# First group of attention without whole query products: the first queries' heads on both row halves, half steps from score 8

## The chip, the cores and the metric

One core of one Trainium2 chip runs the whole program. The metric is device time in microseconds, the median of timed runs. The engines are PE (TensorE: matrix products, with weight loads listed as PEld), ACT (ScalarE), DVE (VectorE), POOL (GpSimd) and SP (SyncE, which here only issues transfers). Each works through its own instructions in order, and they wait for each other by semaphores.

## The reference

A pre-LayerNorm block with multi-query attention (32 heads of 16, one shared key and value head) and a gated feed-forward part:

```python
def _A_ref(x, wq, wk, wv, wo):
    q = (x @ wq).reshape(B, S, H, Dh).transpose(0, 2, 1, 3)
    k = x @ wk
    v = x @ wv
    scores = jnp.einsum("bhqd,bkd->bhqk", q, k) * (Dh ** -0.5)
    p = _softmax(scores, axis=-1)
    o = jnp.einsum("bhqk,bkd->bhqd", p, v)
    return o.transpose(0, 2, 1, 3).reshape(B, S, H * Dh) @ wo

def _B_ref(x, w_gate, w_up, w_down):
    return (_gelu(x @ w_gate) * (x @ w_up)) @ w_down

h = x + _A_ref(_layernorm(x), A_wq, A_wk, A_wv, A_wo)
h2 = h + _B_ref(_layernorm(h), B_w_gate, B_w_up, B_w_down)
```

S is 2048 tokens, D 512, F 1792, everything in float32.

## The kernel before

**Tiling.** The 2048 queries are four blocks of 512 (`b`), the 32 heads are eight groups of four (`g`), the keys sixteen chunks of 128 (`kc`). A *score* is the work of one call of `score(n)`: for two heads, keys of one chunk against 512 queries, two products on PE (L411) into one PSUM tile `s`, followed by one exponential of 128x1024 on ACT (L415) that writes half of a tile `p`. So a group has 32 scores, a block 256; `n` counts them through the program. Two scores (four heads) make one *weighing*: four products with the values into the accumulator `acc` (L419). After a group's last weighing DVE copies `acc` to `oT` (L432), SP stores it to `acc_d` and loads it back in another layout as `oc` (L445), and DVE divides and splits it into `o_hi` and `o_lo`. There is one `acc` bank, and there are three banks for `s`: two with tag `s`, and one, `s3`, for every third score. A score therefore waits for the exponential of three scores earlier.

**Rows.** A product here has only 50 rows of depth: each head's queries are split into a high and a low float32r part, three times 16 rows, plus a row with a bound on the exponent and a row of zeros. `kaug` holds the keys' counterpart twice, in rows 0 to 49 and 64 to 113, so two heads go through the two halves of PE's rows at the same time. Queries take the way through DRAM: `project_q(b, cs, ...)` computes `x @ wq` for 128 columns (eight heads) in PSUM (`pq`), DVE or ACT split it into `qh` and `ql`, SP writes these to `q_d` (L253), and `load_q` reads four heads' 50 rows into `qg` (L391). For block 0 `load_q` puts all four heads into both halves of the rows. The very first group has its own tile `qg_first` (`first_q`, L350, and `first_bound`, L361): heads 0 and 2 in rows 0 to 49, heads 1 and 3 in rows 64 to 113, and nothing in the other halves.

**Projections beside scores.** A projection of 128 columns is 12 *whole products* (four chunks of depth, three terms), or 24 *half steps*, each on 64 of the 128 rows. `scores(..., beside)` (L399) takes two half steps: each goes to one half of the rows, while one head's score product goes through the other half. `project_q` yields `(lane, left, step)` for half steps: first the twelve of lane 0 (rows 0 to 63), then, after DVE has read a mark from the bank, the twelve of lane 1. All products of one projection share one bank `pq` (`psum1`, one buffer in this stage), which DVE copies to `pq_raw` at the end.

**Order.** PE, POOL, ACT, DVE and SP follow the order in which the code is written in this stage. `run` begins group 0 in a loop of its own (from L1064): before certain scores, listed in `RAMP` and then before every fourth, it takes whole products from `later_q`, whose first part is `project_q(1, range(DC), nc.vector, 1, (0, 1))`: columns 0 and 1 of block 1 as whole products, the rest as half steps. In between `q_rest` finishes block 0's own projections (columns 1 to 3: split, store, sums of squares `pqn`, bound `m`). When both are done, a second loop (from L1076) runs plain scores up to score 31 and follows the table `MIXED` from score 32 on: in a period of ten scores, `m` marks one with half steps beside it and `s` a plain one, in runs `mms`, `smm`, `mm`, `ss`, with one or two weighings after each run. `left` counts the half steps still to come and `LAST_Q` (240) the score by which they shall be done.

**Weights.** Beside this `part_weights` goes through 46 pieces of `wo`, `w_gate`, `w_up` and `w_down`: SP loads one (L519), POOL splits it into a high and a low part (L121, L122) and stores both to DRAM (L528, L534). There are four buffers for what is loaded and two for what is stored. At score 256 the early buffers are given up, and SP loads `wo` for the dense part (`load_wo`, L584); this waits for all that still uses those buffers, POOL's stores included. From score 272 on the dense part (projection `pp`, gate, up, down) is woven into the scores of the next block.

Of the kernel before, what the change touches and what calls it, by code (L numbers as in the profile page):

```python
# [9 lines left out]
F32 = mybir.dt.float32  # L10
# [24 lines left out]
LAST_Q = 240  # L35
# [4 lines left out]

HURRY = ((0, 3), (1, 0), (1, 1))

RAMP = {3: 2, 5: 2, 7: 2}

MIXED = {0: ("mms", 2), 3: ("smm", 1), 6: ("mm", 1), 8: ("ss", 1)}

# [4 lines left out]
CUT, EDGE, GAP, HOLD, REST = -1, -2, -3, -4, -5  # L51
# [3 lines left out]
def kernel(  # L55
# [12 lines left out]
    nc = tc.nc  # L68
# [6 lines left out]
    T = 512  # L75
    NT = S // P
    NB = S // T
    TB = T // P
    DC = D // P
    FC = F // P  # L80
    NG = H // 4
    KC = S // P
    HC = P // DH
    KR = 3 * DH + 2
# [25 lines left out]
    q_d = dram.tile([H, KR, S], F32R, name="q_d")  # L110
# [49 lines left out]
    def run(outer, first):  # L160
# [157 lines left out]
        q_rest = project_q(0, range(FIRST_Q, DC), nc.scalar, NB)  # L318

        def later_q():  # L320

            second = project_q(1, range(DC), nc.vector, 1, (0, 1))
            for _ in range(sum(RAMP.values())):
                yield next(second)

            next(q_rest)
            for _ in range(2 * DC - sum(RAMP.values())):
                yield next(second)
            yield from q_rest
            yield 0  # L330
            yield from second
            for b in range(2, NB):
                yield from project_q(b, range(DC), nc.vector, b, ())
            yield REST
            yield REST
            norms.pop()()

        def age():
            for entry in after:
                entry[0] -= 1  # L340
            while after and after[0][0] <= 0:
                after.pop(0)[1]()

        def first_q():

            qg = eb.tile([P, 4, T], F32R, name="qg_first")
            view = q_d.rearrange("h r s -> r h s")
            for a in range(2):
                for r0, r1 in ((3 * DH + 1, KR), (0, 3 * DH)):
                    nc.sync.dma_start(  # L350
                        qg[64 * a + r0 : 64 * a + r1, a::2, :].bitcast(F32),
                        view[r0:r1, a:4:2, :T].bitcast(F32),
                    )
            return qg

        def first_bound(qg):

# [642 lines left out]
        work = None  # L1000
        qgs = {(0, 0): qg_first if first else load_q(0, 0)}
        acc = None
        pend = []

        def finish(n):
            for _ in range(min(n, len(pend))):
                pb, pg, pkc, pp, pacc, _ = pend.pop(0)
                weigh(pacc, pp, pkc)
                if pkc == KC - 1:
                    evacuate(pb, pg, pacc)  # L1010
# [17 lines left out]
        def score(n, beside=()):  # L1028

            nonlocal acc  # L1030
            i, u = divmod(n, 2)
            b, r = divmod(i, PER)
            g, kc = divmod(r, KC)
            if u == 0:
                if kc == 0:
                    cur["qg"] = qgs.pop((b, g))
                    acc = pss.tile([P, T], F32, tag="acc", bufs=1, name=f"acc_{b}_{g}")
                if kc == 2 and b * NG + g + 1 < NB * NG:
                    key = divmod(b * NG + g + 1, NG)
                    qgs[key] = load_q(*key)  # L1040
                cur["p"] = sb.tile([P, 4, T], F32, tag="p", bufs=PB, name=f"p_{i}")
            scores(i, cur["p"], cur["qg"], kc, u, beside)
            if u == 1:
                pend.append((b, g, kc, cur["p"], acc, n))
# [11 lines left out]
        LEAD = (3, 2, 2)  # L1056
        n, lead = 0, 2 * PER + sum(SIZES[: LEAD[0]])
        with tc.manual_schedule(engines={mybir.EngineType.SP, mybir.EngineType.DVE}):
            parts, said = None, 3 if first else 0
            if first:  # L1060
                work = later_q()
                parts = part_weights(early.enter_context(tc.tile_pool(name="parts", bufs=1)))

            while n < 2 * KC and said:  # L1064
                for _ in range(RAMP.get(n, n > 7 and n % 4 == 3) if said else 0):
                    said = next(work)
                    age()
                score(n)
                n += 1
                if n % 4 == 0:  # L1070
                    finish(len(pend) - 2)
                    if parts is not None and n > 12 and n % 24:
                        next(parts)

            token, left = next(work) if first else None, 6 * (NB * DC - 2 - DC) * DC
            while n < lead:  # L1076
                age()
                r = n % (2 * KC)
                if n < 2 * KC or token is None and n % 2 == 0:
                    kinds, runs = "ss", 1  # L1080
                elif r < 30:
                    kinds, runs = MIXED[r % 10]
                else:
                    kinds, runs = ("mm" if left > LAST_Q - n else "ss"), 1
                rest, held = token == REST, False
                if n == 2 * PER:
                    assert token is None
                    while after:
                        age()
                    for _ in parts or ():  # L1090
                        pass
                    if first:
                        check_bound(eb, k2m)
                    parts = work = None
                    early.close()
                    db = late.enter_context(tc.tile_pool(name="dense", bufs=1))
                    load_wo(0)
                for kind in kinds:
                    if kind == "m" and not rest and not held and token not in (None, REST):
                        held = token[1] == 1  # L1100
                        tokens = token, next(work)
                        score(n, [(lane, step) for lane, _, step in tokens])
                        token = next(work, None)
                        left -= 2
                    else:
                        score(n)
                    n += 1
                if n == 2 * PER + 8:
                    primed = dense(0)
                    next(primed)  # L1110
                if rest:
                    token = next(work, None)
                if len(pend) > 2:
                    finish(runs)
                while squares:
                    squares.pop(0)()
                for _ in range(runs):
                    if outs and not pause[0] and n % (2 * KC) not in (2, 3, 4):
                        take_out()
                    pause[0] = max(pause[0] - 1, 0)  # L1120
                if parts is not None and (
                    n % (2 * KC) % 10 in (0, 6) if n > 2 * KC else n // 2 % 5 in (0, 2)
                ):
                    next(parts, None)
            assert n == lead
        assert not outs
        work = primed
# [20 lines left out]
        for c in range(LEAD[0], (NB - 1) * NG * len(SIZES)):  # L1148
            b, cb = divmod(c, NG * len(SIZES))
# [398 lines left out]
```

## Time and profile before

| | us |
|---|---|
| median of 3 timed runs | 1413.45 (1412.93 to 1413.64) |
| the profiled execution, its own time | 1412.15 |
| its span in the profile | 1410.3 |
| scores of group 0, first to last exponential | 51.8 to 84.8 |
| rest of block 0's scores, to the dense part | 84.8 to 312.7 |

In a row of the timeline stand the start, the length, engine, line and operation, what is written from what, the shape and the number of instructions merged into it; in brackets idle time of the engine before it and what ended it. A row of the waits has who waited for what, the microseconds in total, the number of times and the longest. Merged rows overlap a little at their ends, since a product is counted until its last result has left PE; the distance from one start to the next is what an instruction costs its engine. The granted TensorE clock is 1.00 in every stage. `SPq` is SP issuing a transfer; when that has landed shows only in what it releases, and, for POOL's transfers, in the list of transfers.

### The profile page before, as it was taken

The numbers are of one execution on the slowest core, as the hardware profiler recorded it, in microseconds if no ns is written. First come the engines' busy times: TensorE is split into PE (matmuls) and PEld (weight loads), VectorE is DVE, ScalarE is ACT, GpSimd is POOL, SyncE is SP. The second block draws the span as 40 slices with busy tenths as digits, with TensorE's granted clock in tenths as the row PEclk, the third lists the DMA queues.
The fourth block names the chain that finished last, engine by engine and source line by source line (L and its number), as shares of the span: only waits on it lengthen the run. The fifth ranks groups of instructions, "written<-read, shape, count | busy, mean of one in ns | idle before, by whom it ended". The sixth has DMA issues, their size and how long they took to land.

```text
span 1410.3 us, 25577 instructions
## 1 busy us (share of the span) xinstructions
PE 1393.8 (99%) x10622; PEld 780.3 (55%) x10622; DVE 551.3 (39%) x980; ACT 1040.9 (74%) x1149; POOL 184.6 (13%) x278
## 2 busy tenths in 40 slices
PE   9999999999999999999999999999999999999998
PEld 7533333335555555555555555555555555557886
DVE  7421323313342433333252433414352342427665
ACT  7699999996777877777787777877787777772000
POOL 6355556521000000000000000001000000002000
PEclk9999999999999999999999999999999999999999
DMA  4468777752341332233242332223242241435551
GB/s 159 160 203 251 246 259 251 251 192 80 116 150 59 117 117 92 82 99 133 85 169 73 117 117 87 87 95 112 102 146 103 87 147 48 141 123 198 186 194 61
DMA packets 84647, 193.68 MB, mean 137 GB/s; under 512 B 9684, under 2 KB 24020, under 8 KB 84492
## 3 DMA queue, kind: packets, MB, share of 16 engines
q1 hardware_dynamic: 77572, 167.50, 35.5%
q0 software_dynamic: 6784, 24.37, 4.8%
q8 instruction: 85, 1.39, 0.4%
q14 instruction: 38, 0.31, 0.1%
q10 hardware_dynamic: 168, 0.10, 0.0%
HBM read 142.12 MB, written 49.55 MB: 136 GB/s over the span
## 4 chain that ended last, share of the span: by engine, by line
PE 92%; ACT 4%; DMA 2%; DVE 1%; issue 1%; POOL 0%; SPq 0%; DVEq 0%; ACTq 0%; POOLq 0%
PE acc L419 32%; PE s L411 18%; PE pu L933 9%; PE pg L933 8%; PE pd L933 5%; PE pq L409 3%; ACT p L415 3%; PE pd L610 3%; PE pd L632 3%; PE pg L632 3%; PE pu L632 3%; PE pp L610 2%; PE pq L206 1%; DMA x<-in_A_x_dram 1%; PE pp L741 1%; DMA acc_d<-oT 1%
## 5 line engine op out<-in xcount | busy, mean ns | idle before, releaser
L415 ACT ACTIVATE p<-s 128x1024 f32<-128x1024 f32 x1024 | 969.5, 1035 | 226.8 <-PE s L411 223.3
L419 PE MATMUL acc<-p,v_sb 128*32 128x512 f32 x4096 | 494.1, 598 | 0.1
L411 PE MATMUL s<-qg,kaug 50*128 50x512 f32 x1984 | 415.8, 425 | 4.0 <-ACT p L415 3.7
L411 PEld LDWEIGHTS s<-qg,kaug 50*128 50x128 f32 x1984 | 193.0, 184 | 224.5 <-ACT p L415 127.0
L419 PEld LDWEIGHTS acc<-p,v_sb 128*32 128x32 f32 x4096 | 109.7, 109 | 227.5 <-issue 224.4
L933 PE MATMUL pu<-x2h,w 64*128 64x512 f32 x672 | 212.3, 391 | 0.0
L933 PE MATMUL pg<-x2h,w 64*128 64x512 f32 x672 | 211.4, 391 | 0.1
L933 PEld LDWEIGHTS pu<-x2h,w 64*128 64x128 f32 x672 | 116.0, 185 | 14.7
L933 PEld LDWEIGHTS pg<-x2h,w 64*128 64x128 f32 x672 | 115.9, 185 | 14.7 <-DVE g L807 0.5
L933 PE MATMUL pu<-x2l,w 64*128 64x512 f32 x336 | 122.1, 391 | 0.0
L933 PE MATMUL pg<-x2l,w 64*128 64x512 f32 x336 | 122.0, 391 | 0.0
L810 ACT ACTIVATE ga<-ga 128x512 f32<-128x512 f32 x56 | 35.3, 634 | 89.2 <-DVE ga L805 89.2
L131 POOL TENSOR_SCALAR rstd<-mv 128x1 f32<-128x1 f32 x16 | 3.6, 223 | 677.8 <-DVE mv L129 677.7
L933 PE MATMUL pd<-w,gh 64*128 64x512 f32 x384 | 81.2, 392 | 0.0
L875 DVE TENSOR_TENSOR h<-h,pd 128x512 f32<-128x512 f32 x48 | 31.8, 684 | 115.4 <-PE pd L933 66.3
L432 DVE COPY oT<-acc 128x512 f32<-128x512 f32 x32 | 22.1, 691 | 121.2 <-PE acc L419 121.1
L1175 DVE SCALAR_TENSOR_TENSOR ga<-ga,g 128x512 f32<-128x512 f32 x70 | 48.3, 691 | 52.5 <-ACT ga L810 51.5
L459 DVE RECIPROCAL oc<-oc 128x128 f32<-128x128 f32 x64 | 56.8, 924 | 28.9 <-DMA oc<-acc_d 23.7
L794 DVE COPY g<-pg 128x512 f32<-128x512 f32 x56 | 38.7, 692 | 64.0 <-PE pg L933 58.3
L933 PEld LDWEIGHTS pg<-x2l,w 64*128 64x128 f32 x336 | 58.0, 185 | 7.4
L933 PEld LDWEIGHTS pu<-x2l,w 64*128 64x128 f32 x336 | 58.0, 185 | 7.2
L807 DVE SCALAR_TENSOR_TENSOR g<-g,pu 128x512 f32<-128x512 f32 x56 | 38.2, 683 | 40.2 <-PE pu L933 30.3
(244 smaller groups left out, 1436.4 us busy)
## 6 DMA issues: line engine op xcount, KB each, us to landing
w<-w_d SPq DMA_DIRECT2D x112, 512.0 KB
w<-w_d SPq DMA_DIRECT2D x28, 1024.0 KB
qg<-q_d SPq DMA_DIRECT2D x48, 200.0 KB
q_d<-qh SPq DMA_DIRECT2D x32, 256.0 KB
wo<-wo_d SPq DMA_DIRECT2D x8, 1024.0 KB
acc_d<-oT SPq DMA_DIRECT2D x31, 256.0 KB
oc<-acc_d SPq DMA_DIRECT2D x124, 64.0 KB
w_d<-w_0b POOLq DMA_DIRECT2D x14, 512.0 KB, 7.4
```

The costliest lines, as they stand in the source:

```text
L409: step()
L411: nc.tensor.matmul(s[:, a, :], kaug[rows, kc * P : (kc + 1) * P], qg[rows, 2 * u + a, :], start=True, stop=True,)
L415: nc.scalar.activation(p[:, 2 * u : 2 * u + 2, :], s, AF.Exp, scale=SCALE)
L419: nc.tensor.matmul(acc[32 * j : 32 * j + 32, :], v_sb[:, kc, :], p[:, j, :], start=(kc == 0), stop=(kc == KC - 1), skip_group_check=True,)
L459: nc.vector.reciprocal(oc[:, 1, sl], oc[:, 1, sl])
L610: nc.tensor.matmul(banks[k], lhsT[rows], rhs[rows], start=(turn == 0 and i == 0), stop=(turn == 1 and i == n - 1), skip_group_check=True,)
L632: nc.tensor.matmul(bank, lhsT, rhs, start=(i == 0), stop=(i == len(ts) - 1))
L794: nc.vector.tensor_copy(g, pg)
L807: nc.vector.scalar_tensor_tensor(g, g, 0.5, pu, op0=ALU.mult, op1=ALU.mult)
L810: nc.scalar.activation(a, a, AF.Tanh, scale=GELU_A * GELU_C)
L933: nc.tensor.matmul(e["bank"], lhsT[rows], rhs[rows], start=i == 0 and not e["both"], stop=last and e["both"], skip_group_check=True,)
L1175: (soon or lazy).pop(0)()
```

## The change

The own loop of group 0 is gone, with `RAMP`. The second loop runs from score 0: scores 0 to 7 are plain, and from `START = 8` on the table `MIXED` applies, counted from score 8 up to score 27; scores 28 to 31 take the rule of a group's end. All of `later_q` now consists of half steps, those of block 1's columns 0 and 1 included: 288 in place of 240, with no whole products. After score 1 `q_rest` is resumed, and `fill_first` loads the missing halves of `qg_first` from `q_d` (heads 1 and 3 into rows 0 to 49, heads 0 and 2 into rows 64 to 113), two transfers on POOL's queue; after score 5 the rest of `q_rest` runs. A run `ss` becomes `sm` when the half steps still to come are more than 1.2 for each score up to `LAST_Q`. The pieces of weights in group 0 follow the rule of the later groups.

```diff
-RAMP = {3: 2, 5: 2, 7: 2}
+START = 8
...
         def later_q():
 
-            second = project_q(1, range(DC), nc.vector, 1, (0, 1))
-            for _ in range(sum(RAMP.values())):
-                yield next(second)
-
-            next(q_rest)
-            for _ in range(2 * DC - sum(RAMP.values())):
-                yield next(second)
-            yield from q_rest
-            yield 0
-            yield from second
-            for b in range(2, NB):
+            for b in range(1, NB):
                 yield from project_q(b, range(DC), nc.vector, b, ())
...
+        def fill_first():
+
+            view = q_d.rearrange("h r s -> r h s")
+            for a in range(2):
+                nc.gpsimd.dma_start(
+                    qg_first[64 * a : 64 * a + KR, 1 - a :: 2, :].bitcast(F32),
+                    view[:, 1 - a : 4 : 2, :T].bitcast(F32),
+                )
...
-            while n < 2 * KC and said:
-                for _ in range(RAMP.get(n, n > 7 and n % 4 == 3) if said else 0):
-                    said = next(work)
-                    age()
-                score(n)
-                n += 1
-                if n % 4 == 0:
-                    finish(len(pend) - 2)
-                    if parts is not None and n > 12 and n % 24:
-                        next(parts)
-
-            token, left = next(work) if first else None, 6 * (NB * DC - 2 - DC) * DC
+            token, left = None, 6 * (NB - 1) * DC * DC
             while n < lead:
                 age()
-                r = n % (2 * KC)
-                if n < 2 * KC or token is None and n % 2 == 0:
+                r = n % (2 * KC) if n >= 2 * KC else n - START if n < 28 else 30
+                if first and n == START:
+                    token = next(work)
+                if (token is None or token == REST and left <= 0) and (n < START or n % 2 == 0):
                     kinds, runs = "ss", 1
                 elif r < 30:
                     kinds, runs = MIXED[r % 10]
+                    if kinds == "ss" and 5 * left > 6 * (LAST_Q - n):
+                        kinds = "sm"
...
+                if first and n == 2:
+                    next(q_rest)
+                    fill_first()
+                if first and n == 6:
+                    for _ in q_rest:
+                        pass
...
-                if parts is not None and (
-                    n % (2 * KC) % 10 in (0, 6) if n > 2 * KC else n // 2 % 5 in (0, 2)
-                ):
+                if parts is not None and n > 12 and n % (2 * KC) % 10 in (0, 6):
                     next(parts, None)
```

PE around scores 6 to 8. `s_0` and `s_1` are score tiles of heads 0 and 1 or 2 and 3 of a chunk, `pq_0` and `pq_1` block 1's columns 0 and 1 (`xT_hi_85`, `xT_lo_86` are block 1's tokens). Before, from score 6 on:

```order
L411 MATMUL s_0_850<-qg_first,kaug 128x512 x2
L206 MATMUL pq_1_863<-xT_hi_85,wq_hi 128x512
L206 MATMUL pq_1_863<-xT_lo_86,wq_hi 128x512
L206 MATMUL pq_1_863<-xT_hi_85,wq_lo 128x512
L206 MATMUL pq_1_863<-xT_hi_85,wq_hi 128x512
L206 MATMUL pq_1_863<-xT_lo_86,wq_hi 128x512
L206 MATMUL pq_1_863<-xT_hi_85,wq_lo 128x512
L411 MATMUL s_1_870<-qg_first,kaug 128x512 x2
L419 MATMUL acc_0_803<-p_804,v_sb 32x512 x4
L419 MATMUL acc_0_803<-p_813,v_sb 32x512 x4
L411 MATMUL s_0_883<-qg_first,kaug 128x512 x2
```

And after the change, from score 5 on (`pqn` are the sums of squares of block 0's columns 1 to 3):

```order
L410 MATMUL s_1_841<-qg_first,kaug 128x512 x2
...
L263 MATMUL pqn_1_845<-qs_3_817,sel 32x512
L418 MATMUL acc_0_803<-p_804,v_sb 32x512 x4
L410 MATMUL s_0_859<-qg_first,kaug 128x512 x2
L410 MATMUL s_1_863<-qg_first,kaug 128x512 x2
L418 MATMUL acc_0_803<-p_824,v_sb 32x512 x4
L408 MATMUL pq_0_877<-xT_hi_85,wq_hi 128x512
L410 MATMUL s_0_879<-qg_first,kaug 128x512
L408 MATMUL pq_0_877<-xT_lo_86,wq_hi 128x512
L410 MATMUL s_0_879<-qg_first,kaug 128x512
L408 MATMUL pq_0_877<-xT_hi_85,wq_lo 128x512
```

The whole products of block 1 between the scores are gone; the first half step of block 1 stands beside score 8, which is the first to read the filled halves of `qg_first`, and the sums of squares have moved from score 18 to score 5.

POOL after its last work on `kaug`. Before, then with the change (`mm`, `m` are the bound of block 0's heads 8 to 31, `wo0b` is the first piece of weights):

```order
L1362 TENSOR_TENSOR kaug<-vT_688,kaug 16x512 x2
L121 CAST wo0b<-wo0r 128x512
L122 TENSOR_TENSOR wo0b<-wo0r,wo0b 128x512
L534 DMA wo_d<-wo0b 128x1024
L121 CAST wo1b<-wo1r 128x512
L122 TENSOR_TENSOR wo1b<-wo1r,wo1b 128x512
L273 TENSOR_SCALAR mm_1_981<-q_70,k2m 32x1
```
```order
L1358 TENSOR_TENSOR kaug<-vT_688,kaug 16x512 x2
L350 DMA qg_first<-q_d 50x2x512 x2
L273 TENSOR_SCALAR mm_1_852<-q_70,k2m 32x1
...
L290 TENSOR_SCALAR m_1_853<-qn_1_849,mm_1_852 32x512
L294 DMA q_d<-m_1_853 24x512
L121 CAST wo0b<-wo0r 128x512
```

The two fills stand directly behind the work on `kaug`, and the bound stands ahead of the weights instead of among them.

SP from group 1's load of queries on, before and with the change (`wo0r` to `w20r` are loads of pieces of weights):

```order
L391 DMA qg_1_829<-q_d 50x4x512 x2
L253 DMA q_d<-qh_0_854 8x16x512
...
L253 DMA q_d<-qh_3_896 8x16x512
L519 DMA wo0r<-in_A_wo_dram 128x512
L519 DMA wo1r<-in_A_wo_dram 128x512
...
L519 DMA w_0r<-in_B_w_gate_dram 128x4x128
L436 DMA acc_d<-oT_0_1128 128x512
L391 DMA qg_2_1136<-q_d 50x4x512 x2
L445 DMA oc_0_1131<-acc_d 16x2x512 x4
L519 DMA w_1r<-in_B_w_up_dram 128x4x128
```
```order
L390 DMA qg_1_833<-q_d 50x4x512 x2
L518 DMA wo0r<-in_A_wo_dram 128x512
L518 DMA wo1r<-in_A_wo_dram 128x512
L518 DMA wo2r<-in_A_wo_dram 128x512
L253 DMA q_d<-qh_0_1024 8x16x512
...
L518 DMA w_0r<-in_B_w_gate_dram 128x4x128
L518 DMA w_1r<-in_B_w_up_dram 128x4x128
L435 DMA acc_d<-oT_0_1136 128x512
L390 DMA qg_2_1144<-q_d 50x4x512 x2
L444 DMA oc_0_1139<-acc_d 16x2x512 x4
L518 DMA w20r<-in_B_w_down_dram 128x512
```

The first weights are no longer behind the stores of block 1's first projection, and `w_1r` has moved ahead of group 0's store and what follows it.

2 lines of the change are left out of this document (1 added, 1 removed).

## The prediction, as put on record before the changed kernel ran

> **What bounds the kernel now.** I read the page's busy table and the chain that ended last, then busy time by stage (before the first exponential, group 0, the rest of block 0 with products beside it, its end without, everything after), then the timelines of ACT, PE, POOL and SP where stages meet. Page and stages (columns: busy of PE, PEld, DVE, ACT, POOL with counts, granted clock, DMA share, GB/s):
>
> ```profile
> span 1410.3 us, 25577 instructions
> PE 1393.8 (99%) x10622; PEld 780.3 (55%) x10622; DVE 551.3 (39%) x980; ACT 1040.9 (74%) x1149; POOL 184.6 (13%) x278
> PE 92%; ACT 4%; DMA 2%; DVE 1%; issue 1%; POOL 0%; SPq 0%; DVEq 0%; ACTq 0%; POOLq 0%
> ...
> 51.80:84.80 33.00, 32.01 (x209) 12.56 (x205) 8.24 (x13) 29.96 (x32) 12.47 (x16) 1.00 0.62 213
> 84.80:275.10 190.30, 190.11 (x1446) 72.49 (x1444) 54.34 (x76) 186.38 (x201) 106.15 (x132) 1.00 0.77 245
> 275.10:312.70 37.60, 36.81 (x244) 10.82 (x242) 8.31 (x13) 36.64 (x41) 11.45 (x17) 1.00 0.59 195
> 312.70:1410.30 1097.60, 1087.26 (x8462) 646.75 (x8462) 442.41 (x791) 754.51 (x823) 21.77 (x44) 1.00 0.33 114
> ```
>
> PE is the bound nearly everywhere, ACT close behind in block 0. The change touches only what stands before 312.70. In group 0 ACT is idle for 33.00 - 29.96 = 3.04 us: an upper bound on what an even start can give there. ACT's timeline says where, and what it needs when nothing holds it:
>
> ```profile
> 51.79 6.62 ACT L415 ACTIVATE p<-s 128x1024 f32<-128x1024 f32 x7 [0.71 <-PE s L411]
> ...
> 61.40 3.77 ACT L415 ACTIVATE p<-s 128x1024 f32<-128x1024 f32 x4 [1.28 <-PE s L411]
> ...
> 77.58 7.44 ACT L415 ACTIVATE p<-s 128x1024 f32<-128x1024 f32 x8 [0.21 <-PE s L411]
> ...
> 280.81 34.02 ACT L415 ACTIVATE p<-s 128x1024 f32<-128x1024 f32 x37 [0.96 <-PE s L411]
> ```
>
> Undisturbed, 37 exponentials take 34.02 us, 0.92 each (0.91 from start to start among the first seven). The 1.28 is PE being late with a score.
>
> **The change part by part.** *Prices.* PE's timeline, first in group 0 (six whole products, one score, two weighings, the next scores), then one period of ten scores in a later group:
>
> ```profile
> 56.95 0.50 PE L206 MATMUL pq<-xT_hi,wq_hi 128*128 128x512 f32 x1 [0.28 <-DVE pq_raw L227]
> ...
> 58.55 0.50 PE L411 MATMUL s<-qg_first,kaug 50*128 50x512 f32 x2
> 58.98 1.92 PE L419 MATMUL acc<-p,v_sb 128*32 128x512 f32 x16
> 60.84 0.96 PE L411 MATMUL s<-qg_first,kaug 50*128 50x512 f32 x6
> ...
> 83.75 0.50 PE L409 MATMUL pq<-xT_hi,wq_hi 64*128 64x512 f32 x1
> ...
> 93.49 0.49 PE L409 MATMUL pq<-xT_hi,wq_hi 64*128 64x512 f32 x1
> ...
> 99.12 0.50 PE L409 MATMUL pq<-xT_hi,wq_lo 64*128 64x512 f32 x1
> ...
> 100.25 1.07 PE L419 MATMUL acc<-p,v_sb 128*32 128x512 f32 x8
> 101.24 0.73 PE L411 MATMUL s<-qg,kaug 50*128 50x512 f32 x4
> 101.91 1.07 PE L419 MATMUL acc<-p,v_sb 128*32 128x512 f32 x8
> 102.90 0.49 PE L409 MATMUL pq<-xT_hi,wq_hi 64*128 64x512 f32 x1
> ```
>
> From start to start: six whole products 58.55 - 56.95 = 1.60, so 0.27 each; a lone score 58.98 - 58.55 = 0.43; two scores with half steps beside both 100.25 - 99.12 = 1.13; two plain scores 101.91 - 101.24 = 0.67; a weighing 0.99. A score with its two half steps thus costs PE 0.23 more than a plain one. Two half steps do the work of one whole product: the removed 24 cost 24 x 0.27 = 6.4 us, the added 24 scores' worth of half steps 24 x 0.23 = 5.5. PE's work falls by 0.9 us; the rest of the gain can only come from PE standing idle less. Ten scores with six such pairs take 102.90 - 93.49 = 9.41 us, 0.94 a score against ACT's 0.92: PE bounds the mixed rhythm by a hair, plain scores with weighings (0.67 + 0.99 = 1.66 for two) leave it slack of 0.17 for two.
>
> *Start.* Score 7 needs the buffer of exponential 4, which starts at 51.79 + 4 x 0.91 = 55.43 and ends 1.04 later, at 56.5. Score 7 (0.43) and one weighing (0.99) follow, so PE stands before score 8 at 57.9; now score 8 begins at 60.84. The sums of squares (three small products), moved ahead to score 5, fall into the time in which PE waits for ACT there.
>
> *Scores 8 to 31.* Before, score 32 begins at 83.75. Now 24 scores with 17 pairs: 24 x 0.94 = 22.6 with 14.4 pairs, plus 2.6 x 0.23 = 0.6, is 23.2; 57.9 + 23.2 = 81.1. Gain here 2.65 us.
>
> *What is owed.* Counted in PE's order, scores 32 to 231 carry 121 pairs instead of 120 (+0.2 us), scores 232 to 240 carry 6 where none were: 6 x 0.23 = 1.4 us on PE, of which 9 x 0.085 = 0.8 lay idle, so +0.6. Together 0.8. Gain at score 272, where the dense work starts: 2.65 - 0.8 = 1.85 us if nothing waits.
>
> *The added transfer.* Score 8 takes both heads from rows 64 up, and head 0 lies there only after the second fill of qg_first (2 x 50 x 2 rows of 2 KB, 200 KB each), issued on POOL's queue. Behind the fills on that queue stands the bound of heads 8 to 31, which now goes ahead of the first weights; group 2 needs it at score 36, so it has time. Rows for its price: POOL's last work before it, the spread of landing for POOL's smallest stores (64 and 48 KB), and two of its 512 KB ones:
>
> ```profile
> 49.94 4.32 POOL L1362 TENSOR_TENSOR kaug<-vT,kaug 16x512 fp32r<-16x512 f32 x3
> ...
> DMA to landing us min/median/max: 1.9/2.5/6.8
> ...
> wo_d<-wo1b POOLq DMA_DIRECT2D x1, 512.0 KB, 3.0
> ...
> w_d<-w21b POOLq DMA_DIRECT2D x1, 512.0 KB, 9.6
> ```
>
> POOL is free at 49.94 + 4.32 = 54.3; with some 0.6 to issue the first, the second goes out at 55.0 and lands between 1.9 and 9.6 later: 56.9 to 64.6. I take 3.5, between the small median 2.5 and the large ones, since SP moves query rows then (share 0.62 above): 58.5, so PE waits 0.6 at score 8. Behind it in PE's queue stand all later scores and weighings, so with PE the bound this is lost whole. Gain 1.85 - 0.6 = 1.25.
>
> The Trainium skill (DMA: Bandwidth & Descriptors, "Anatomy of one DMA — SWDGE (gpsimd) path") gives about 2.0 us plus bytes over 436 GB/s for such a transfer; by that estimate the second fill lands after 2.5 us, at 57.5, nothing waits, and the sum would be 1.85. The trace agrees at its best store (3.2 by the rule, 3.0 measured) and not at its slow ones (9.6), so I keep the rows.
>
> *Where the gain must pass.* At the end of block 0 the chain of waits leaves PE. Rows: POOL's weights chain at its start, a stall in it, its end; SP's load of wo; the chain; PE's wait in it:
>
> ```profile
> 73.07 0.61 POOL L121 CAST wo0b<-wo0r 128x512 fp32r<-128x512 f32 x1 [18.81 <-DMA wo1r<-in_A_wo_dram]
> ...
> 100.51 0.60 POOL L121 CAST w_1b<-w_1r 128x512 fp32r<-128x512 f32 x1 [8.69 <-DMA w_1r<-in_B_w_up_dram]
> ...
> 297.69 0.57 POOL L294 DMA_DIRECT2D q_d<-m  x1 [0.29 <-POOL m L290]
> ```
> ```profile
> 299.90 0.90 SPq L584 DMA_DIRECT2D wo<-wo_d  x2
> ```
> ```profile
> 300.87 0.70 DVE oT L432
> 301.59 6.87 DMA acc_d<-oT
> ...
> 316.29 0.44 DVE o_hi L470
> ...
> 316.77 0.73 PE pp L610 x2
> ```
> ```profile
> PEld pp L610 <- DVE o_hi L470: 0.5, 1, 0.5
> ```
>
> PE's projection waits for the last group's output, whose 256 KB store takes 6.87 us right behind the two 1 MB loads of wo; these go out once POOL's last store (297.69) has landed. If they stay at 299.9, an earlier PE only waits longer at 316.77 and the gain is gone. I expect them earlier: wo1r (landing at 73.07) now goes out ahead of the three 256 KB stores of block 1's first projection, some 2 us sooner; and w_1r stands before the group's store on SP instead of behind it, so the 8.69 us stall comes one weight piece later, worth (297.69 - 73.07) / 46 = 4.9 us for one of 46 pieces. Against that, 400 KB of fills and 768 KB of query rows fall into the busy stretch: 1.17 MB at 245 GB/s, 4.8 us. Bounds of the shift: -6.9 to +4.8; I take -2, which lets the 1.25 through. All else keeps its order and DMAs; from 312.70 on no instruction moves.
>
> *Sum.* 1410.3 - 1.25 = 1409.05 for the span. The profiled execution took 1412.15, 1.85 around its span, and the median of the timed runs is 1413.45: forecast **1412.2 us**.
>
> **Rivals.** (a) *The fill lands in time and the end of block 0 loosens too:* 1.85 plus the 0.5 of PE's wait, and up to the 3.04 of group 0 if the debt stays hidden: 2.4 to 3.5, so 1411.1 to 1409.9, the middle at 1410.4. For it: PE waits for nothing but ACT elsewhere in group 0. Against: PE's mixed rhythm has no room for the debt. (b) *The gain is swallowed:* wo's load does not move, PE waits at the projection as long as it came early; 1413.45. For it: 316.77 is on the chain already. (c) *The fill is late:* at 9.6 us it lands at 64.6, PE stands 6.7 before score 8, ACT runs dry: 1413.45 - 1.85 + 6.7 = 1418.3. No gain from 59.75 on, slower by over 0.2% from 62.6. For it: stores of 512 KB at 9.6; against: the share was 0.62, not the 0.77 of later. (d) *The weights end later:* the 4.8 us of added transfers outweigh the earlier start, wo, the store and the projection all slip by 4.8: 1418.2; it decides from any slip, since PE waits there now. (e) *The products were no cost:* PE does nearly the same work, and without less idle time only the 0.9 of cheaper steps is left: 1412.55, inside the forecast.
>
> **How the numbers follow.** Forecast with (e) 0.42, (a) 0.24, (b) 0.13, (c) 0.11, (d) 0.10. The likeliest case's own range is 1411.2 to 1413.2. The 8-in-10 range leaves out the far halves of (c) and (d) and the tail of (a): 1410.0 to 1416.6. A measurement of this kernel tells about 0.2% (2.8 us, so 1410.6 and 1416.3) from no change. Faster by more is the better two thirds of (a): 0.16. Slower by more is the greater part of (c) and (d), 0.17, and 0.03 for what I do not see: 0.20. Between: 0.64.
>
> **What would show it.** ACT's first run unbroken over about 8 exponentials, one gap before the ninth of at most 0.6, none from 61 to 78; score 32 near 81.7 instead of 83.75; the last half steps near score 240; wo's load before 299 and the projection's wait at most 0.5. The forecast is wrong if PE idles over 2 us before score 8 (c), if wo's load goes out after 300 (b, d), or if PE's ten-score period in groups 0 to 7 differs from 9.41.

## The result, and the profile after

The changed kernel takes 1416.53 us (median of 8 runs, 1415.30 to 1420.65); the kernel before took 1412.98 in the same comparison (8 runs, 1411.96 to 1413.68). The ratio is 1.0029, with a 95% interval of 1.0018 to 1.0040: it became slower by 3.55 us, where 1.25 us less had been forecast. The profiled execution took 1415.30, its span 1413.6, 1.7 around it.

By stage (busy of PE, PEld, DVE, ACT, POOL, then the granted clock, DMA share and GB/s), cut where the same scores begin as in the rows of before:

```profile
span 1413.6 us, 25632 instructions
...
51.80:87.30 35.50, 31.58 (x219) 11.71 (x215) 6.51 (x11) 30.08 (x32) 14.11 (x19) 0.90 0.56 182
87.30:277.80 190.50, 190.50 (x1448) 73.38 (x1448) 51.82 (x79) 186.03 (x200) 108.71 (x135) 1.00 0.81 254
277.80:315.40 37.60, 37.19 (x258) 11.71 (x256) 10.36 (x17) 37.23 (x41) 7.63 (x12) 1.00 0.54 188
315.40:1413.60 1098.20, 1087.04 (x8462) 646.43 (x8462) 440.69 (x789) 754.18 (x823) 21.78 (x44) 1.00 0.32 114
```

All of it is in group 0: 35.50 us for its 32 exponentials instead of 33.00. The other stages are as long as before within 0.6 us. And the granted clock, 1.00 in every stage of before, is 0.90 there. ACT's timeline shows where:

```profile
51.79 5.61 ACT L414 ACTIVATE p<-s 128x1024 f32<-128x1024 f32 x6 [0.71 <-PE s L410]
61.20 1.94 ACT L414 ACTIVATE p<-s 128x1024 f32<-128x1024 f32 x2 [3.80 <-PE s L410]
64.03 4.92 ACT L414 ACTIVATE p<-s 128x1024 f32<-128x1024 f32 x5 [0.90 <-PE s L410]
```

The first run breaks off after six exponentials and not after eight, with 3.80 us of waiting for PE. What PE did in that time, with DVE, which it waits for, and POOL, which issues the added transfers:

```profile
55.13 0.61 PE L263 MATMUL pqn<-qs,sel 128*32 128x512 bf16 x2
58.14 0.59 PE L263 MATMUL pqn<-qs,sel 128*32 128x512 bf16 x1 [2.40 <-DVE qs L248]
58.25 2.18 PE L418 MATMUL acc<-p,v_sb 128*32 128x512 f32 x8
60.36 1.22 PE L410 MATMUL s<-qg_first,kaug 50*128 50x512 f32 x4
61.51 1.79 PE L418 MATMUL acc<-p,v_sb 128*32 128x512 f32 x8
63.23 0.50 PE L408 MATMUL pq<-xT_hi,wq_hi 64*128 64x512 f32 x1
```
```profile
56.33 0.43 DVE L121 CAST qh<-pq_raw 128x512 fp32r<-128x512 f32 x1 [5.92 <-DMA q_d<-qh]
56.79 0.69 DVE L122 TENSOR_TENSOR ql<-pq_raw,qh 128x512 fp32r<-128x512 f32 x1
57.40 0.68 DVE L248 TENSOR_TENSOR qs<-qh 128x512 bf16<-128x512 f32 x1
```
```profile
54.17 1.63 POOL L350 DMA_DIRECT2D qg_first<-q_d  x2
```
```profile
DMA to landing us min/median/max: 6.9/7.5/8.1
...
qg_first<-q_d POOLq DMA_DIRECT2D x2, 200.0 KB, 7.5
```

Three things stand in these rows.

- The third of the sums of squares, column 3's, finds its operand missing: DVE's `qh` of that column needs a buffer (there are two) that column 1's store still holds. That store was issued at 50.25 and lands 5.96 us later, so `qs` is there at 58.1, and PE idles 2.40 us in front of the product. All that PE has to do next, scores 6 and 7 included, stands behind it.
- The fills go out at 54.17 and 0.9 later and take 6.9 and 8.1 us: they land at 61.1 and 63.1. Score 8, which needs the second, begins at 63.23. The trace names no wait there, because PE comes to it at the same moment.
- From 58.25 to 63.23, 4.98 us, PE does two weighings (eight rows of the trace each) and, between them, two scores, which cost 0.99 + 0.67 + 0.99 = 2.65 at the rates of the prediction. That is the granted clock:

```profile
52.00:56.00 4.00, 2.21 (x10) 0.77 (x9) 0.00 (x0) 4.00 (x5) 3.71 (x4) 1.00 0.52 177
56.00:60.00 4.00, 1.86 (x9) 0.41 (x8) 2.92 (x5) 1.40 (x2) 0.00 (x0) 0.52 0.62 201
60.00:64.00 4.00, 4.00 (x22) 1.45 (x20) 0.15 (x1) 1.94 (x2) 2.70 (x6) 0.62 0.58 211
```

PE is busy 2.21 of 4 us even before the wait, since the whole products that filled this time are gone; then the clock is half for 6.83 us, from 56.2 to 63.0. In the kernel before PE has no gap in those first 4 us:

```profile
52.00:54.00 2.00, 2.00 (x10) 1.34 (x10) 0.00 (x0) 2.00 (x3) 1.93 (x2) 1.00 0.55 192
54.00:56.00 2.00, 2.00 (x12) 1.12 (x8) 0.00 (x0) 2.00 (x3) 0.26 (x1) 1.00 0.49 171
```

From score 8 to score 32 the new rhythm takes 87.31 - 64.03 = 23.28 us.

### The profile page after: what moved, and what is told of

The parts are those of the page before. It is cut to its first block, busy times and chain, and to the rows that moved or that the text cites. A ratio compares the mean times of both kernels' runs of the same rounds, so it can differ in the third digit from the quotient of the medians.

```text
span 1413.6 us, 25632 instructions
## 1 busy us (share of the span) xinstructions
PE 1393.2 (99%) x10646; PEld 780.2 (55%) x10646; DVE 547.4 (39%) x982; ACT 1040.9 (74%) x1149; POOL 185.0 (13%) x280
## 4 chain that ended last, share of the span: by engine, by line
PE 92%; ACT 3%; DMA 1%; DVE 1%; issue 1%; POOL 1%; SPq 0%; ACTq 0%; DVEq 0%; POOLq 0%
PE acc L418 33%; PE s L410 18%; PE pu L932 8%; PE pg L932 8%; PE pd L932 5%; PE pq L408 4%; PE pd L609 3%; PE pd L631 3%; PE pg L631 3%; PE pu L631 3%; ACT p L414 2%; PE pp L609 2%; PE pp L740 1%; PE pxt L676 1%; DMA x<-in_A_x_dram 0%
## 5 line engine op out<-in xcount | busy, mean ns | idle before, releaser
L793 DVE COPY g<-pg 128x512 f32<-128x512 f32 x56 | 38.8, 692 | 63.2 <-PE pg L932 57.5
```

The source lines that it names most:

```text
L793: nc.vector.tensor_copy(g, pg)
```

## The experiments

Fifteen kernels, in four batches. Theories: **A**, only the sums of squares hold PE before score 8; **B**, only the fill does; **AB**, each is enough; **C**, the half steps themselves cost the time later. After the first batch came **D** (the half clock follows from PE's idle time in scores 0 to 7), **G** (the dense start swallows any lead, since `acc_d` stands behind `wo`), later **G2** (it needs both `wo` and the last `oc` by the time PE comes to them), and **H**, which is C for the dense stage.

The measure for most is how far behind or ahead a run's profile, one execution of each kernel, is of the kernel before, where the same exponential begins: scores 8 and 32, score 272 (the dense work starts) and 280, and the last. Positive is later. Beside it the time at half clock near score 8 and at the dense start.

| run | median us | before us | ratio (95%) | 8 | 32 | 272 | 280 | last | half clock |
|---|---|---|---|---|---|---|---|---|---|
| the change | 1416.53 | 1412.98 | 1.0029 (1.0018-1.0040) | +2.63 | +2.48 | +2.70 | +2.72 | +2.99 | 6.83, 0 |
| e1 | 1422.06 | 1412.76 | 1.0061 (1.0048-1.0074) | +2.34 | +5.13 | +5.54 | +5.57 | +6.33 | 10.24, 0 |
| e2 | 1419.48 | 1412.76 | 1.0051 (1.0038-1.0064) | +4.70 | +4.54 | +4.57 | +4.63 | +5.20 | 10.24, 0 |
| e3 | 1416.98 | 1412.76 | 1.0030 (1.0018-1.0042) | -1.34 | -1.14 | -0.90 | +5.60 | +5.26 | 3.41, 6.83 |
| e4 | 1417.27 | 1412.76 | 1.0034 (1.0022-1.0046) | -2.39 | -2.97 | -2.07 | +3.54 | +3.97 | 0, 3.41 |
| e5 | 1414.87 | 1413.52 | 1.0001 (0.9987-1.0015) | -0.01 | 0.00 | -0.02 | -0.02 | +1.75 | 0, 0 |
| e6 | 1417.77 | 1413.52 | 1.0026 (1.0011-1.0042) | -1.63 | -2.04 | -1.38 | +3.94 | +5.13 | 3.41, 6.83 |
| e7 | 1417.45 | 1413.52 | 1.0015 (1.0000-1.0031) | +0.09 | +1.48 | +1.90 | +6.19 | +7.73 | 10.24, 6.83 |
| e8 | 1416.33 | 1413.52 | 1.0008 (0.9994-1.0022) | -2.40 | -2.09 | -1.85 | +1.73 | +4.12 | 0, 3.41 |
| e9 | 1414.88 | 1413.08 | 1.0007 (0.9996-1.0018) | -0.07 | -0.09 | -0.23 | +2.87 | +3.56 | 0, 3.41 |
| e10 | 1413.94 | 1413.08 | 1.0002 (0.9987-1.0016) | -2.43 | -3.01 | -2.36 | -0.70 | +0.39 | 0, 0 |
| e11 | 1414.28 | 1413.08 | 1.0001 (0.9987-1.0015) | -0.95 | -1.53 | -0.86 | -0.27 | +1.89 | 3.41, 0 |
| e12 | 1414.83 | 1413.08 | 1.0007 (0.9991-1.0023) | -1.12 | -0.90 | -0.61 | +0.92 | +2.28 | 3.41, 3.41 |
| e13 | 1413.28 | 1412.84 | 0.9993 (0.9980-1.0005) | -0.25 | -0.60 | +0.06 | +0.08 | +1.17 | 6.83, 0 |
| e14 | 1411.93 | 1412.84 | 0.9986 (0.9974-0.9998) | -1.12 | -1.81 | -0.94 | -0.94 | +0.33 | 3.41, 0 |
| e15 | 1411.31 | 1412.84 | 0.9985 (0.9975-0.9995) | -2.26 | -1.71 | -1.49 | -1.48 | -0.87 | 0, 0 |

The ratios are of means; among the runs of before in the last three batches are a few of 1417 to 1422, which weigh in them, so medians stand beside.

### One wait taken away, the other, both

**e1_late_squares**: the sums of squares of block 0's columns 1 to 3 wait until block 1's first projection ends.

```diff
-            if halves:
+            if halves or not urgent:
                 norms.append(norm)
                 return
```

> The three products that sum the squares of block 0's columns 1 to 3 go from score 5 to the end of block 1's first projection (score 25); the fill stays on POOL's queue. Theory A (only these products hold PE, since they wait for DVE until 58.14): score 8 begins near 57.9 instead of 63.23, time 5.3 us under the changed kernel, about 1411.2. Theory B (only the fill holds PE; it landed at 63.16) and theory AB (each of the two is enough): PE now waits for the fill alone, score 8 still begins at 62.5 to 63.5, time about 1416.5. Theory C (the loss comes from the half steps themselves): score 8 earlier, but the time stays at 1416.5.

**e2_early_fill**: the second halves of `qg_first` are loaded on SP right behind the first, before the scores; their row of bounds follows as four small transfers from `m`; the call of `fill_first` is gone.

```diff
+            for a in range(2):
+                for r0, r1 in ((3 * DH + 1, KR), (0, 3 * DH)):
+                    nc.sync.dma_start(
+                        qg[64 * a + r0 : 64 * a + r1, 1 - a :: 2, :].bitcast(F32),
+                        view[r0:r1, 1 - a : 4 : 2, :T].bitcast(F32),
+                    )
...
-                    fill_first()
```

> The fill goes out on SP right behind the first load of qg_first (43 us) and with four small bound rows, nothing on POOL; the squares stay at score 5. Theory A and AB: the squares' products still wait for DVE, score 8 at 62.5 to 63.5, about 1416.5. Theory B: score 8 near 58 to 59, about 1411.5. Theory C: 1416.5.

**e3_both**: both edits.

> Late squares and early fill together. Theories A, B and AB: nothing waits, score 8 near 57.9, score 32 near 81.1, and the forecast's gain of 1.85 us against the kernel before appears: about 1411.2 to 1411.6. Theory C: no better than 1416.

**e4_start14**: neither; half steps begin at score 14 and the rest of `q_rest` comes after score 11, so that both have time.

```diff
-START = 8
+START = 14
...
-                r = n % (2 * KC) if n >= 2 * KC else n - START if n < 28 else 30
+                r = n % (2 * KC) if n >= 2 * KC else n - START if n < 29 else 30
...
-                if first and n == 6:
+                if first and n == 12:
                     for _ in q_rest:
```

> Half steps begin at score 14 and the squares are summed after score 11; the fill stays on POOL's queue. Both waits are then over when PE gets there. AB, A and B: PE never idles over 1 us in group 0, score 14 near 63.4, score 32 near 80.7 with some 5 pairs of half steps more to do later (5 x 0.23 = 1.2 us): 1.3 us under the kernel before, about 1411.7. Theory C: 1416.

Each wait is enough to hold PE. PE's timeline of e1, without the sums of squares in the way, and of e2, without the fill:

```profile
62.52 0.76 PE L410 MATMUL s<-qg_first,kaug 50*128 50x512 f32 x1 [2.73 <-DMA qg_first<-q_d]
```
```profile
60.44 0.59 PE L263 MATMUL pqn<-qs,sel 128*32 128x512 bf16 x1 [4.07 <-DVE qs L248]
```

In e2 the wait even grew, as the four small transfers on SP push the stores of `qh` and `ql` back: the store that DVE waits for went out 2.5 us later. In time both missed the 1416.5 that AB expected, by 5.6 and 3.0 us: both had 10.24 us at half clock, in e1 in two pieces, the second behind the wait for the fill. With both gone (e3) score 8 comes 1.34 us earlier than before, and with half steps from score 14 (e4) ACT isn't interrupted at all:

```profile
51.76 14.88 ACT L414 ACTIVATE p<-s 128x1024 f32<-128x1024 f32 x16 [0.70 <-PE s L410]
```

So AB holds for the start. But the times did not fall: e3 and e4 are 0.90 and 2.07 us ahead at score 272 and 5.60 and 3.54 behind at score 280. PE of e4 at that place, by its timeline, then four-microsecond stretches, then the chain of waits:

```profile
319.00 1.22 PE L609 MATMUL pp<-wo,o_hi 64*128 64x512 f32 x4 [4.29 <-DVE o_hi L469]
```
```profile
316.00:320.00 4.00, 1.00 (x4) 0.84 (x6) 3.57 (x6) 0.00 (x0) 0.00 (x0) 0.87 0.96 354
320.00:324.00 4.00, 4.00 (x28) 1.39 (x28) 0.16 (x1) 1.94 (x2) 0.00 (x0) 0.71 0.77 310
```
```profile
295.46 5.39 DMA q_d<-m
...
301.21 0.39 SPq L583
...
302.98 7.72 DMA acc_d<-oT
...
312.03 2.17 DMA oc<-acc_d
...
318.52 0.44 DVE o_hi L469
```

`oT` was ready at 299.5, but its store stands on SP behind the loads of `wo`, which wait for POOL's store of `m`, and then shares the DMA engines with their 2 MB. PE arrives early, idles 4.29 us, and gets 3.4 us of half clock on top: more than the lead is lost. C has nothing for it: the lead is constant but for some 0.2 to 0.9 us from score 32 to 272, and lost at one place.

### The order of SP's transfers at the dense start, and the clock

**e5_before_acc**, **e6_start14_acc**, **e7_both_acc**: the kernel before, e4 and e3, with the loads of `wo` behind the store, the `oc` loads and the next queries.

```diff
-                    load_wo(0)
...
+                if n == 2 * PER + 6: load_wo(0)
                 if n == 2 * PER + 8:
                     primed = dense(0)
```

> The kernel before, with one order changed on SP at the end of block 0: the two 1024 KB loads of wo are issued after the last acc_d store, its four oc loads and the next queries' load, and no longer ahead of them. Theory G (the dense start is a gate: acc_d waits behind wo, which waits for the store of m, so that PE can't have the last o_hi before about 317 to 320 us, however early it is): the kernel before has no wait there (its longest PE wait at 312 to 314 us is 0.42), so nothing to gain: 1412.8 plus or minus 0.6; slower, up to 1416, if wo now lands after 313.9, where the first products with it stand. Theory H (the half steps beside scores cost the time later on by themselves): the same 1412.8.

> The run with half steps from pair 14, with the same order on SP. It stood 2.07 us ahead of the kernel before at score 272 and 3.54 behind at score 280, after a PE wait of 4.29 us for o_hi and 3.4 us at half clock. Theory G: o_hi is there in time, the lead stays: score 280 about 2 us earlier than before, no half clock at 319, time 1410.7 (1410.0 to 1411.6). Theory H: the order on SP changes nothing, 1417.

> The run with early fill and late sums of squares, with the same order on SP. It stood 0.90 us ahead at score 272 and 5.6 behind at score 280. Theory G: 1411.9 (1411.2 to 1412.7). Theory H: 1417. In scores 0 to 7 its PE has little to do, so theory D (a window of 3.4 us in which PE was busy some 60% of the time or less is followed by one at half clock) expects a half clock of 3.4 us near 56 us again, and score 8 near 60.

**e8_both_warm_acc**: e7, with the products of scores 2 to 6 done twice.

```diff
-                nc.tensor.matmul(
+                for _ in range(2 if 2 <= 2 * i + u <= 6 else 1):
+                    nc.tensor.matmul(
...
```

> As the run with early fill, late sums of squares and the new order on SP, but the matmuls of scores 2 to 6 are done twice into the same bank, so that PE is busy while it would wait for ACT. Theory D: the clock stays at 1.0 from 50 to 65 us, score 8 starts at 58.2 to 58.7 and no longer at 60.06, and the time is 1.4 us below the run without the repeats: 1410.5 (1409.8 to 1411.4). If the clock falls for another reason, or the repeats hold up ACT: score 8 at 60 or later, 1412 or more.

The dense start stayed shut, for the opposite reason. `o_hi` was early now (310.51 in e8) and `wo` late; PE of e8:

```profile
314.30 1.22 PE L621 MATMUL pp<-wo,o_hi 64*128 64x512 f32 x4 [2.60 <-DMA wo<-wo_d]
```

The times that G expected of e6, e7 and e8 were missed by 5.6 to 7.1 us; the control e5 kept its place up to score 280 and lost some 1.8 us later on, so that its median lies 1.35 above that of the kernel before. D fits this pair: up to score 256, e7 and e8 differ only in the repeats, and e7 has half clock for 10.24 us and score 8 at 61.49, e8 none and score 8 at 59.00. But each is one execution, and e3, the same program as e7 up to score 256, had 3.41 us and score 8 at 60.06.

**e9_before_wo2**, **e10_start14_wo2**, **e11_start14_warm_wo2**, **e12_both_warm_wo2**: the loads of `wo` right behind the store of `oT`, ahead of the `oc` loads; on the kernel before, on e4, on e4 with the repeats, on e3 with them.

```diff
                 nc.sync.dma_start(acc_d[:, g % 4, :], oT)
+            if b == 0 and g == NG - 1: load_wo(0)
...
-                    load_wo(0)
```

> The kernel before with another order on SP at the end of block 0: the last acc_d store first, then the two wo loads, then the oc loads. Theory G2 (the dense start needs both wo and the last oc by the time PE comes to them; in the kernel before both are just in time): no lead to keep, 1413.0 plus or minus 0.8. Control for the runs below.

> Half steps from pair 14, with that order on SP. Theory G2: wo is issued near 301 us and landed by 308, oc landed by 308 and o_hi there by 313, so that PE finds both and keeps its lead of 1.4 to 2.1 us at score 280: 1411.2 (1410.4 to 1412.6; the upper part where the clock falls near 55 us, as it did in one of two profiles). Theory H (the lead is lost in the dense stage whatever the order): 1416.5 to 1417.5.

> The same with the matmuls of scores 2 to 6 done twice. Theories D and G2 together: no half clock near 55 us in any run, score 32 some 2.5 to 3 us ahead of the kernel before, score 280 some 2 us ahead, 1410.8 (1410.0 to 1411.8), below both kernels, and a narrower spread than without the repeats. Theory H: 1416 or more.

> Early fill, late sums of squares, scores 2 to 6 done twice, with that order on SP. With wo behind oc this stood 1.85 us ahead at score 272 and 1.73 behind at score 280, after a PE wait of 2.60 us for wo at 314 and 3.4 us at half clock. Theory G2: no such wait, 1411.1 (1410.3 to 1412.2). Theory H: 1416.

e10 takes 3.3 us less than e4, with the order of three transfers alone. It keeps 0.70 of 2.36 us; the `oc` loads now go out beside `wo`, and PE waits 1.83 us for `o_hi`. For the kernel before (e9) the new order is a loss of 3 us at this place, so its own is fitted to its own times. And e11 and e12 show that the repeats don't always hold the clock: both had 3.41 us of half clock in spite of them. The times that G2 expected of e10, e11 and e12 were missed by 2.7 to 3.7 us.

### The loads of wo split, and PE's own work moved

**e13_start14_split**: e4, with one half of `wo` right behind the store of `oT` and the other behind the `oc` loads.

```diff
                 nc.sync.dma_start(acc_d[:, g % 4, :], oT)
+            if b == 0 and g == NG - 1: load_wo(0, (0,))
...
             elif not last:
                 turn_out()
+                if b == 0: load_wo(0, (1,))
...
-                    load_wo(0)
```

**e14_start14_lag_split**: also, in the first scores, weighings one pair behind the scores and no longer two. **e15_both_lag_split**: both edits on e3, that is the change without its two waits.

```diff
-                if len(pend) > 2:
+                if len(pend) > (1 if n < 12 else 2):
```

> Half steps from pair 14; on SP at the end of block 0: acc_d, the first half of wo, the four oc loads, the second half of wo. Theory G2 (only these transfers take the lead): oc lands some 2 us earlier than with all of wo ahead of it, o_hi is there by 314.5, PE doesn't wait for it, score 280 is about 2 us ahead of the kernel before (0.70 with all of wo ahead): 1412.5 (1411.3 to 1413.6). Rival (the lead is lost to something else in the dense stage, later at the latest): score 280 at most 0.7 us ahead, 1414 or more.

> The same, and in the first twelve scores the weighted sums of a pair of scores follow one pair behind and no longer two. Theory D: PE's first sums stand near 53.5 instead of 55.1, no stretch of 3.4 us from 49 to 60 has PE busy less than 0.75, the clock stays at 1.0 there; score 32 is 3 us ahead of the kernel before in every run, and the spread is narrower: 1411.8 (1410.8 to 1413). If the clock has nothing to do with idle time: half clock near 55 in some of the runs as before, 1412.5 and a wide spread.

> Early fill, late sums of squares, half steps from pair 8 as in the change, weighted sums one pair earlier, wo split. Theories D and G2: this is the change with its two waits, its idle start and the gate at the dense start taken away, so it should give about what was forecast for it: score 8 near 58.5, score 32 at 82, 1412.0 (1411.0 to 1413.2). If a loss of the change is still hidden elsewhere: 1414 or more.

The split opens the dense start: e14 and e15 keep 0.94 of 0.94 and 1.48 of 1.49 us. e13 had no lead to keep, as its profile fell on 6.83 us of half clock; and e14, too, had 3.41 us of it, after a window of 3.41 us with PE busy 0.59 of it, which ended 0.6 us after the first weighing began, so the earlier weighings alone don't rule it out. In e15's chain of waits the store of `oT` takes 3.81 us and PE begins the projection with no wait for `o_hi` or `wo`:

```profile
300.09 3.81 DMA acc_d<-oT
...
312.41 1.65 PE pp L622 x12
```

The earlier weighings fill PE's first microseconds with its own work. Here is e15 in stretches; in the same two the change has PE busy 1.32 and 3.86 us, at a clock of 0.77 and 0.50:

```profile
54.00:58.00 4.00, 4.00 (x30) 1.17 (x24) 0.00 (x0) 4.00 (x5) 0.15 (x1) 1.00 0.52 180
58.00:62.00 4.00, 4.00 (x32) 1.39 (x26) 1.72 (x3) 3.99 (x5) 0.00 (x0) 1.00 0.53 202
```

e15 is the fastest kernel of the study: 1411.31 (12 runs, 1410.39 to 1413.71), 1.5 us below the median of the kernel before and 5.2 below the change. By the ratio, 0.9985 (0.9975 to 0.9995), it is faster than before, though by less than the 0.2% that one measurement can tell; without the three runs of before over 1419 the ratio is 0.9988. Its lead stands at 1.38 us by score 256, ahead of the split loads, so it does not come from them. How much of it comes from the earlier weighings isn't shown, since they were not tried on the kernel before.

**What the half clock costs.** e4, e6, e10 and e13 are the same program up to score 256, four profiles of it. ACT of e13, to be held against the unbroken row of e4:

```profile
51.78 5.60 ACT L414 ACTIVATE p<-s 128x1024 f32<-128x1024 f32 x6 [0.70 <-PE s L410]
58.12 1.94 ACT L414 ACTIVATE p<-s 128x1024 f32<-128x1024 f32 x2 [0.73 <-PE s L410]
61.15 3.77 ACT L414 ACTIVATE p<-s 128x1024 f32<-128x1024 f32 x4 [1.10 <-PE s L410]
```
```profile
54.00:58.00 4.00, 3.58 (x16) 0.99 (x14) 1.72 (x3) 3.39 (x4) 1.82 (x3) 0.53 0.58 194
```

In e4 the same stretch has the same 3.58 us of PE, at clock 1.00 and with 26 products in place of 16. At score 32 the four are 2.97, 2.04, 3.01 and 0.60 ahead, with 0, 3.41, 0 and 6.83 us at half clock. Nothing else differs in their code, so 3.41 us at half clock cost 0.9 here and 6.83 cost 2.4.

## Why the prediction was wrong

**The start is the step that failed.** The prediction put PE before score 8 at 57.9, and the sums of squares "fall into the time in which PE waits for ACT there". They cost PE little, but one had an operand that wasn't ready: 2.40 us of waiting, behind a chain that the prediction never followed (buffer of `qh`, store of column 1, 5.96 us). PE came to score 8 at 63.23, 5.3 late. e1 to e3 show that this wait is real and, by itself, enough. Where nothing holds the start, in e15, PE comes to score 8 at 58.37, half a microsecond behind the 57.9, and the lead at score 272 is 1.49 us of the 1.85: the sum was near, and the operand was missing from it.

**The fill was mis-sized.** Taken at 3.5 us, landing at 58.5; measured 6.9 and 8.1, landing at 63.1, inside the bounds of 56.9 to 64.6. The rows nearest to it were the slow ones, 6.8 among the small stores and 9.6, not the small median of 2.5. The list of transfers has nine stores of 256 KB of SP's between 46 and 64 us, a likely cause that no run took away. The Trainium skill (DMA: Bandwidth & Descriptors, "Anatomy of one DMA — SWDGE (gpsimd) path") gives an estimate of 2.5 us; the trace differs by a factor of three, and the measurement decides. Rival (c) was this term, with its price: from 1413.45, less the gain of 1.85, plus 5.3, it gives 1416.9, and 1416.53 was measured. That this comes so near is in part luck, since (c) had neither the operand nor the clock in it. The two waits and the slow clock all end near 63.2 and hide each other, so the 5.3 isn't divided among them; without any one the others would have held PE nearly as long (e1 and e2 for the waits; at full clock, by this estimate, PE would have been ready at 58.25 + 2.65 = 60.9, and the fill would have held it).

**The clock was no term at all.** The rows of before show 1.00 everywhere, and the prediction priced every instruction at that. The 24 whole products kept PE busy while ACT set the pace; the 0.9 us saved in PE's work, which no run measures by itself, came with idle time at the start, and that brings half clock. The step "PE standing idle less" as the source of the gain missed that PE's idle time was moved to the front of the group. That idle time there brings the half clock rests on the count of windows below; e7 against e8 and e15 fit it, one execution each.

**The rhythm was near.** Scores 8 to 32 were put at 23.2 us and took 23.28, though 23.98 in e15; e4's ACT runs sixteen exponentials in 14.88, 0.93 each. What is owed later was put at 0.8, too much for the change: from score 32 to 272 it loses 0.2, as do e3 and e15. e4, which begins its half steps six scores later and owes more, loses 0.9.

**Where the gain must pass** was the right place and the wrong size. POOL's last store of weights did move, from 294.26 to 286.93, even more than the bound of 6.9. But `wo` waits for the store of `m` behind it. POOL's work for that now waits 4.46 us for DVE; the store still goes out 2.95 us earlier than before, at 294.74 instead of 297.69, but takes 4.9 us to land instead of 2.0, so that it lands at 299.6 in both:

```profile
291.97 0.26 POOL L273 TENSOR_SCALAR mm<-q,k2m 32x1 f32<-32x1 f32 x1 [4.46 <-DVE q L268]
...
294.74 0.57 POOL L294 DMA_DIRECT2D q_d<-m  x1 [0.29 <-POOL m L290]
```
```profile
300.01 0.90 SPq L583 DMA_DIRECT2D wo<-wo_d  x2
```

So the load of `wo` went out at 300.01, 0.1 later than before, not 2 earlier. Why the store took longer was not tried. For the change this cost nothing, since it came late anyway. With the start mended it is rival (b), and worse than that: (b) had the gain swallowed, and e3 and e4 lost 6.5 and 5.6 us at this place, where a wait of over 4 us was followed by half clock. With leads of 0.90 and 2.07 us at score 272 these two ended at 1416.98 and 1417.27: mending the start alone would not have brought the forecast.

Rivals (a) and (e) fell with the start. (d) didn't happen in the change; in e3 and e4 the load of `wo` went out at 303.38 and 301.21, so that (d)'s slip has a part in their loss. The signs that were named held up: ACT's first run broke, the load of `wo` was after 300, and PE idled over 2 us before score 8.

## What to carry to other kernels

Before moving an instruction forward, follow its operand back: not only the engine that writes it, but the buffer that this engine writes into and the transfer that must leave it first. Work that fills PE's waiting time may be what holds its clock; taking it out is priced by what PE does in each stretch of a few microseconds, not by the sum. And a lead is worth what the next gate lets through: look at what is queued ahead of the transfer that the gate waits for, and try the start and the gate together. Here neither the start alone (e3, e4) nor another order alone (e5, e9) brought a gain.

## What the runs showed that was not expected

**The clock's windows.** In all seventeen profiles, half clock came in pieces of 3.41, 6.83 or 10.24 us, multiples of 3.41, on a grid whose phase differs from one execution to the next. Take PE's busy time, by its rows, in each window of 3.41 us of that grid, without the last 30 us of each program. Among some 6800 windows at full clock, none with PE busy over 0.76 was followed by half clock (18 drops), and every one below 0.59 was; of those from 0.59 to 0.76, 7 of 40 were. In the last microseconds, where PE runs out of work, the lower figure does not hold: three windows with 0.45, 0.53 and 0.58 were not followed by half clock. The Trainium skill (TensorE: Matmul & The Clock Gate, "Part 1: The HAM clock gate") states a free-running window of 3413 ns, and the trace agrees with its 3.41; it puts the low state down to an idle window, while here PE was busy 0.55 to 0.76 of the window in ten of the drops. The phase tells the same program's profiles apart: the windows from about 49 to 56 us had PE busy 0.62 and 0.71 in e4 and 0.63 and 0.71 in e10, with no drop, while one beginning near 51 us had 0.55 in e6 and 0.59 in e13, with one. Laid anywhere between 44 and 66 us, a stretch of 3.41 us has PE busy 0.78 or more in the kernel before; in the change every phase leaves a window there with less than 0.53. In e14 and e15 only a window that begins from 49.4 to 50.4 is below 0.60: e14 had such a window, e15 had not, so that e15's full clock in its profile is in part luck. Wide times fit this: e7's twelve runs go from 1412.16, with a granted clock of 0.999 over the run, to 1420.05, with 0.993; e15's from 1410.39 to 1413.71.

**Small transfers among large ones.** In the change POOL's two loads of 200 KB took 6.9 and 8.1 us, beside SP's stores of 256 KB at a DMA share near 0.6, and its store of 48 KB at 63.02 took 8.1, at a share of 0.5 to 1.0; before, the store of 48 KB took 1.9.

**What stays open.** Between 0.59 and 0.76 the busy share doesn't tell whether the clock falls; busy time in these rows is modelled, and the limit may lie in something else that goes with it. And e15 and e14 lose some 1 us of their lead in the dense stage. So do other kernels with another order of transfers, e5 1.8 us without any change to its half steps, while the change, with the order of before, loses 0.3: so the half steps (theory H) need not be the cause. In e15 one wait of PE, which the kernel before does not have, is at the place, and what makes DVE late there was not tried:

```profile
PE pg L945 <- DVE g L819: 0.9, 1, 0.9
```
